# First loads of a transformer kernel re-queued: key weights on ScalarE's DMA queue, x blocks and q0 on SyncE's, with holds

## Chip, cores, metric

The kernel runs on one core of a Trainium2 chip. The metric is device time in microseconds (us) of one execution, as the median over the executions of a round. A profile of one execution gives its span (first to last instruction), which is about 1.8 us less than the device time. "Landed" is the moment when a transfer's completion is signalled.

Engines: PE is TensorE (matmuls), PEld its weight loads, DVE is VectorE, ACT is ScalarE, POOL is GpSimd, SP is SyncE. The loads told of here are issued by SP and ACT (in the profile of before from 0.74 and 0.76 us on); SP's queue is q1 in the profile and ACT's q10.

## The reference, cut to what matters

Four layers over x of 2048 rows by 1024 columns (bfloat16): linear attention, gated MLP, and both again.

```python
x = x + _A_ref(_layernorm(x), A_wqkv, A_wo)          # linear attention
x = x + _B_ref(_layernorm(x), W_gate, W_up, W_down)  # gated MLP
x = x + _A_ref(_layernorm(x), A_wqkv, A_wo)
x = x + _B_ref(_layernorm(x), W_gate, W_up, W_down)
```

Only the start of the first layer matters here: layer-norm of the first four x blocks (128 rows each, x0 to x3) and their products with the two halves of the key weights, k0 and k1 (columns 0 to 511 and 512 to 1023 of the keys).

## The kernel before

The head of the first layer issues the loads and then interleaves, block by block, statistics and scaling on VectorE, transposes and matmuls on TensorE.

```python
# head(): ten idle matmuls on zeros first, then the loads
k0, k1, v0, q0, q1 = (ring.place() for _ in range(5))   # each load goes to SyncE's queue
self.load_x(0, 0, nc.scalar)       # first half of x0, 128 KB
self.load_x(0, 1)                  # second half
self.load_x(1, None, nc.scalar)    # x1, 256 KB
k0(0, H)                           # first half of k0, 512 KB
self.load_x(2, None, nc.scalar)
k0(H, 2 * H)
self.load_x(3, None, nc.scalar)
k1()                               # 1024 KB
q0()
self.load_x(4) ...                 # cut: x5 to x7, q1, x8 to x15, v0
```

```python
# head_units(): the order on each engine, block 0 (x0) and what follows
def block0():
    stat(0, 0); stat(0, 1); rstd(0)      # VectorE; rstd also two steps on ScalarE
    stat(1, 0)                           # x1's statistics fill the wait for rstd(0)
    scale(0, 0); scale(0, 1)             # VectorE
    t0 = turn(0, 0); t1 = turn(0, 1)     # TensorE transposes
    t0("s"); stat(1, 1); rstd(1); t1("v")
    k(0, 0, between)                     # x0 times k0; x1's scaling and transposes in between
# then: block1 = x1 times k0, k(0, 1) = x0 times k1, transposes of x2, k(1, 1), k(2, 0),
# transposes of x3, k(2, 1), k(3, 0), k(3, 1)
```

In all traces here DMAs are issued in the order of their engine's program (SyncE's at 0.74, 1.19 and 1.66 us), and VectorE runs its instructions in the order written, which this kernel fixes by hand. So `scale(0, 0)` doesn't start before `stat(1, 0)` has had x1 (in the first profile of before x1 landed at 5.19, `stat(1, 0)` began at 5.22 and `scale(0, 0)` at 5.90).

Of the kernel before, what the change touches and what calls it, by code (L numbers as in the profile page):

```python
# [18 lines left out]
class _Ring:  # L19
# [9 lines left out]
    def place(self):  # L29

        name, src = self.plan[self.loaded]
        t = self.pool.tile([P, 8, NW], BF16, tag="w")
        self.tiles[name] = t
        self.loaded += 1
        return lambda lo=0, hi=8: self.nc.sync.dma_start(out=t[:, lo:hi, :], in_=src[:, lo:hi, :])

    def load_to(self, n):
        while self.loaded < min(n, len(self.plan)):
# [40 lines left out]
class _Net:  # L79
# [131 lines left out]
    def head(self):  # L211

        nc, tc, ring = self.nc, self.tc, self.ring
        H = self.KT // 2

        zero = self.ep.tile([P, NW], BF16, tag="e")
        nc.vector.memset(zero, 0.0)
        idle = self.ps3.tile([P, NW], F32, tag="b")
        for _ in range(10):
            nc.tensor.matmul(idle, lhsT=zero[:, 0:P], rhs=zero, start=True, stop=True)  # L220

        k0, k1, v0, q0, q1 = (ring.place() for _ in range(5))
        self.load_x(0, 0, nc.scalar)
        self.load_x(0, 1)
        self.load_x(1, None, nc.scalar)
        k0(0, H)
        self.load_x(2, None, nc.scalar)
        k0(H, 2 * H)
        self.load_x(3, None, nc.scalar)
        k1()  # L230
        q0()
        self.load_x(4)
        self.load_x(5)
        self.load_x(6)
        self.load_x(7)
        q1()
        for t in range(8, self.ST):
            self.load_x(t)
        v0()
        src = self.xb  # L240
        self.xnT[0, 0] = self.xnTp.tile([P, self.KT, QT * P], BF16, tag="xnT", name="xnT0_0")
        stats = [self.small.tile([P, 2, nc.vector.BN_STATS_DIM], F32, tag="stats", name=f"st{j}")
                 for j in range(QT)]
        rs, xn = {}, {}

        def stat(j, c):
            self.ln_stat(j, src[j], c, stats[j])

        def rstd(j):
            rs[j] = self.ln_rstd(stats[j])  # L250
            xn[j] = self.xn_home(0, j)

        def scale(j, h=None):
            self.ln_scale(src[j], *rs[j], xn[j], h)

        def turn(j, h):
            tp = self.ps3.tile([P, H, P], BF16, tag="b")
            for i in range(H):
                kt = h * H + i
                nc.tensor.transpose(tp[:, i, :], xn[j][:, kt * P:(kt + 1) * P], self.ident)  # L260
            dst = self.xnT[0, 0][:, h * H:(h + 1) * H, j * P:(j + 1) * P]

            def take(engine):
                if engine == "v":
                    nc.vector.tensor_copy(out=dst, in_=tp)
                else:
                    nc.scalar.activation(out=dst, in_=tp, func=ACT.Copy)

            return take

        return stat, rstd, scale, turn

    def head_units(self, k, stat, rstd, scale, turn):

        def block0():
            stat(0, 0)
            stat(0, 1)
            rstd(0)
            stat(1, 0)
            scale(0, 0)  # L280
            scale(0, 1)
            t0 = turn(0, 0)
            t1 = turn(0, 1)
            t0("s")
            stat(1, 1)
            rstd(1)
            t1("v")
            k(0, 0, between)

        def between():  # L290

            scale(1, 0)
            t0 = turn(1, 0)
            scale(1, 1)
            t0("v")

        def block1():
            turn(1, 1)("v")
            norm(2)
            k(1, 0)  # L300

        def norm(j):
            stat(j, 0)
            stat(j, 1)
            rstd(j)

        def block(j, c, n):
            scale(n)
            t0 = turn(n, 0)
            t1 = turn(n, 1)  # L310
            t0("s")
            t1("s")
            if n + 1 < QT:
                norm(n + 1)
            k(j, c)

        return [block0, block1, lambda: k(0, 1), lambda: block(1, 1, 2), lambda: k(2, 0),
                lambda: block(2, 1, 3), lambda: k(3, 0), lambda: k(3, 1)]

# [62 lines left out]
    def layer_A(self, l, last_ln):  # L382
        nc, G, KT, D = self.nc, self.G, self.KT, self.D
        ring, later = self.ring, self.later
        H = D // NW
# [155 lines left out]
        def column_major(f, q):  # L541
            return [lambda j=j, c=c: f(q, j, c) for c in range(H) for j in range(QT)]
# [4 lines left out]
        def run(*lists):  # L547

            n = max(len(u) for u in lists)
            for i in range(n):  # L550
                for u in lists:
                    if i < len(u):
                        u[i]()
                        later.tick()
# [12 lines left out]
        def quarter0():  # L567
            self.phi_lag = 3 if l == 0 else 0
            run(first)
            run(column_major(q_unit, 0))  # L570
            later.at(1, lambda: None)
            self.phi_lag = 0

        if l == 0:
            with self.tc.manual_schedule(engines={mybir.EngineType.DVE,
                                                  mybir.EngineType.Activation}):
                quarter0()
        else:
            run(first, column_major(q_unit, 0))
# [160 lines left out]
```

## Time and profile before

| | before |
|---|---|
| median of 4 executions (range) | 1629.32 us (1629.21 to 1630.51) |
| the profiled execution: time, span | 1630.68, 1628.9 us |
| TensorE busy | 1621.7 us |
| TensorE idle before the fifth k matmul | 1.73 us, until k0's second half landed |

Read it so: TensorE is full but for some 7 us, so only what moves the start of its unbroken work can move the end. The lines stand in the prediction.

### The profile page before, as it was taken

To read this page: it belongs to the slowest core of one execution; us is meant where nothing else is said; L and a number is where in the kernel's file an instruction comes from. 1 tells how busy PE (TensorE), PEld (TensorE's weight loads), DVE (VectorE), ACT (ScalarE), POOL (GpSimd) and SP (SyncE) were. 2 spreads that over 40 slices of the span, in tenths; PEclk is the share of its full clock that TensorE was granted. 3 is DMA by queue.
4 is the path that set the end of the run, shared out by engine and by line. 5 is a ranking of instruction groups with operands and counts; after the bars stand their busy time and mean duration, and the time that the engine had idled before them with its cause. 6 is when DMAs were issued, how large, how long until landed. Compare 5 with 4: busy or idle time off the path is not lost.

```text
span 1628.9 us, 18772 instructions
## 1 busy us (share of the span) xinstructions
PE 1621.7 (100%) x7754; PEld 739.3 (45%) x7754; DVE 566.7 (35%) x940; ACT 331.8 (20%) x638; POOL 201.9 (12%) x134
## 2 busy tenths in 40 slices
PE   8999999999999999999999999999999999999999
PEld 4444444444444444444444444444444444444444
DVE  7845695213212222212165547942022111111211
ACT  5741212101110110111066312121011101101110
POOL 2349220000000000000023592100000000000000
DMA  7312647448445444544560147464554454454452
GB/s 245 65 52 56 178 71 206 144 148 232 155 143 190 160 151 161 168 147 137 168 128 1 53 93 250 85 193 146 182 165 152 155 184 155 145 166 154 155 162 71
DMA packets 298246, 235.06 MB, mean 144 GB/s; under 512 B 101296, under 2 KB 294192, under 8 KB 298160
## 3 DMA queue, kind: packets, MB, share of 16 engines
q1 hardware_dynamic: 292832, 228.75, 47.7%
q10 hardware_dynamic: 5328, 5.11, 0.9%
q8 instruction: 60, 0.98, 0.3%
q14 instruction: 26, 0.21, 0.0%
HBM read 201.33 MB, written 8.39 MB: 129 GB/s over the span
## 4 chain that ended last, share of the span: by engine, by line
PE 98%; ACT 1%; DVE 1%; DMA 1%; issue 0%; SPq 0%; DVEq 0%
PE pu L639 24%; PE pg L639 24%; PE acc L663 23%; PE ps L404 12%; PE ps L530 7%; PE ps L439 7%; DMA t<-in_A_wqkv_dram 1%; PE kv L452 0%; PE acc_last L663 0%; ACT e L351 0%; ACT e L350 0%; PE fold L515 0%; DVE st L138 0%; ACT e L352 0%; DVE slab L358 0%
## 5 line engine op out<-in xcount | busy, mean ns | idle before, releaser
L639 PEld LDWEIGHTS <-t 128*128 128x128 bf16 x3584 | 350.3, 98 | 423.2
L639 PE MATMUL pu<-xnT,t 128*128 128x512 bf16 x1792 | 423.5, 379 | 0.0
L639 PE MATMUL pg<-xnT,t 128*128 128x512 bf16 x1792 | 423.4, 379 | 0.0
L663 PE MATMUL acc<-t,hT 128*128 128x512 bf16 x1764 | 382.5, 379 | 0.0
L645 DVE TENSOR_TENSOR hT<-pu,rg 128x512 bf16<-128x512 f32 x224 | 154.7, 691 | 572.0 <-PE pu L639 572.0
L644 ACT ACTIVATE rg<-pg 128x512 f32<-128x512 f32 x224 | 133.5, 596 | 737.3 <-PE pg L639 737.0
L663 PEld LDWEIGHTS <-hT 128*128 128x128 bf16 x1820 | 177.9, 98 | 209.1
L404 PE MATMUL ps<-t,xnT 128*128 128x512 bf16 x1024 | 224.3, 380 | 2.2 <-DMA t<-in_A_wqkv_dram 1.7
L404 PEld LDWEIGHTS <-xnT 128*128 128x128 bf16 x1024 | 99.2, 98 | 122.3 <-issue 4.3
L530 PE MATMUL ps<-T,pqT 128*128 128x512 bf16 x512 | 111.2, 379 | 0.0
L145 ACT ACTIVATE rstd<-mv,eps 128x1 f32<-128x1 f32 x64 | 18.7, 293 | 334.1 <-DVE mv L143 333.9
L680 DVE TENSOR_TENSOR xo<-x,acc 128x512 bf16<-128x512 f32 x31 | 21.3, 688 | 170.3 <-PE acc L663 170.3
L483 POOL TENSOR_TENSOR prod<-pq,zrow 128x1024 f32<-128x1024 bf16 x32 | 67.9, 2122 | 85.9 <-DVE den L488 72.5
L138 DVE BATCH_NORM_STATS2 stats<-x 128x6 f32<-128x512 f32 (+1 forms) x120 | 78.0, 673 | 0.8
L530 PEld LDWEIGHTS <-pqT 128*128 128x128 bf16 x512 | 49.9, 98 | 60.4 <-issue 0.5
L419 POOL CAST ksum<-x 128x512 f32<-128x512 bf16 x2 | 1.7, 866 | 605.4 <-DVE x L358 605.4
L677 DVE TENSOR_TENSOR x<-x,acc 128x512 f32<-128x512 f32 x32 | 21.6, 675 | 138.5 <-PE acc L663 137.4
L421 POOL TENSOR_TENSOR ksum<-ksum,slab 128x512 f32<-128x512 f32 x46 | 54.0, 1183 | 84.6 <-DVE slab L358 75.1
L358 DVE SCALAR_TENSOR_TENSOR pq<-ps,e 128x512 bf16<-128x512 f32 x64 | 44.0, 688 | 53.9 <-ACT e L352 52.2
L495 POOL TENSOR_TENSOR pq<-pq,den 128x1024 bf16<-128x1024 bf16 x32 | 61.7, 1933 | 3.1 <-DVE den L490 3.1
L488 DVE TENSOR_REDUCE den<-prod 128x32 f32<-128x1024 f32 x32 | 39.0, 1217 | 53.9 <-POOL prod L483 53.9
L439 PE MATMUL ps<-slab,x 128*128 128x512 bf16 x256 | 56.6, 379 | 0.0
(57 smaller groups left out, 596.0 us busy)
## 6 DMA issues: line engine op xcount, KB each, us to landing
t<-in_B_W_gate_dram SPq DMA_DIRECT2D x56, 1024.0 KB, 7.1
t<-in_B_W_up_dram SPq DMA_DIRECT2D x56, 1024.0 KB, 5.4
t<-in_B_W_down_dram SPq DMA_DIRECT2D x64, 896.0 KB, 5.2
t<-in_A_wqkv_dram SPq DMA_DIRECT2D x11, 1024.0 KB, 5.6
t<-in_A_wo_dram SPq DMA_DIRECT2D x4, 1024.0 KB, 7.2
away<-x SPq DMA_DIRECT2D x8, 512.0 KB, 4.4
x<-away SPq DMA_DIRECT2D x8, 512.0 KB, 8.5
out_dram<-xo ACTq DMA_DIRECT2D x31, 128.0 KB, 2.5
```

The source lines that it names most:

```text
L138: self.nc.vector.bn_stats(out=stats[:, c, :], in_=src[:, c * fmax:(c + 1) * fmax])
L358: nc.vector.scalar_tensor_tensor(out=out, in0=ps, scalar=0.0, in1=e, op0=ALU.max, op1=ALU.add)
L404: nc.tensor.matmul(by_row(ps), lhsT=self.xnT[l, l_q][:, kt, j * P:(j + 1) * P], rhs=w[:, kt, :].rearrange("p (b i d) -> p i b d", i=R, d=H ...
L421: nc.gpsimd.tensor_tensor(out=ksum[:, cols], in0=ksum[:, cols], in1=pk, op=ALU.add)
L439: nc.tensor.matmul(ps, lhsT=self.xn[l, t][:, d * P:(d + 1) * P], rhs=self.pk[l, t][:, h * NW:(h + 1) * NW], start=(t == 0), stop=(t == sel ...
L483: nc.gpsimd.tensor_tensor(out=prod, in0=pq_of[sc, j], in1=zrow, op=ALU.mult)
L495: nc.gpsimd.tensor_tensor(out=heads(pq), in0=heads(pq), in1=den[:, :].unsqueeze(2).to_broadcast([P, D // HD, HD]), op=ALU.mult)
L530: nc.tensor.matmul(ps, lhsT=pqT[sc][:, g, j * P:(j + 1) * P], rhs=T[g // 2][:, g % 2, n2 * NW:(n2 + 1) * NW], start=(g == 0), stop=(g == G ...
L639: nc.tensor.matmul(ps, lhsT=w[:, kt, fi * P:(fi + 1) * P], rhs=self.xnT[l, q][:, kt, :], start=(kt == 0), stop=(kt == KT - 1))
L644: nc.scalar.activation(out=rg, in_=pg, func=ACT.Relu)
L645: nc.vector.tensor_tensor(out=h[:, fi, :], in0=pu, in1=rg, op=ALU.mult)
L663: nc.tensor.matmul(ps[:, 0:n], lhsT=hT[ft // 4][:, ft % 4, j * P:(j + 1) * P], rhs=wd[:, k, i * n:(i + 1) * n], start=(ft == 0), stop=(ft ...
```

## The change

Its intent: k0 should not have to share the DMA engines with x2 and x3, which are needed later (in the profile of before SyncE's queue moved 0.44 MB from 5.5 to 8 us and ScalarE's 0.43). So k0 and k1 get ScalarE's queue, held by a tiny memset into k0's tile until the first x block is on its way; the first x blocks have SyncE's; x2 is held by a memset into its tile that VectorE runs only after the first statistics of x0. In the same move q0 comes directly behind x3 on SyncE's queue, where it used to stand behind k1.

```diff
         k0, k1, v0, q0, q1 = (ring.place() for _ in range(5))
-        self.load_x(0, 0, nc.scalar)
+        self.load_x(0, 0)
         self.load_x(0, 1)
-        self.load_x(1, None, nc.scalar)
-        k0(0, H)
-        self.load_x(2, None, nc.scalar)
-        k0(H, 2 * H)
-        self.load_x(3, None, nc.scalar)
-        k1()
-        q0()
-        self.load_x(4)
...
+        self.load_x(1)
+
+        nc.vector.memset(ring.get((0, "k0"))[:, 0, 0:2], 0.0)
+        k0(0, H, nc.scalar)
+        k0(H, 2 * H, nc.scalar)
+        k1(0, 2 * H, nc.scalar)
+
+        def rest():
+            nc.vector.memset(self.xb[2][:, 0:2], 0.0)
+            self.load_x(2)
+            self.load_x(3)
+            q0()
+            for t in range(4, 8):
+                self.load_x(t)
...
         def block0():
             stat(0, 0)
+            rest()
             stat(0, 1)
```

(Cut: passing `rest` and the queue argument through, and SyncE in the list of engines whose order is kept by hand.)

More of the change, by code (lines that the diff above doesn't have):

```diff
@@ L34, in place @@
         self.loaded += 1
-        return lambda lo=0, hi=8: self.nc.sync.dma_start(out=t[:, lo:hi, :], in_=src[:, lo:hi, :])
+        return lambda lo=0, hi=8, queue=None: (queue or self.nc.sync).dma_start(
+            out=t[:, lo:hi, :], in_=src[:, lo:hi, :])
     def load_to(self, n):
@@ L222, in head @@
         k0, k1, v0, q0, q1 = (ring.place() for _ in range(5))
-        self.load_x(0, 0, nc.scalar)
+        self.load_x(0, 0)
         self.load_x(0, 1)
-        self.load_x(1, None, nc.scalar)
-        k0(0, H)
-        self.load_x(2, None, nc.scalar)
-        k0(H, 2 * H)
-        self.load_x(3, None, nc.scalar)
-        k1()
-        q0()
-        self.load_x(4)
-        self.load_x(5)
-        self.load_x(6)
-        self.load_x(7)
-        q1()
-        for t in range(8, self.ST):
-            self.load_x(t)
-        v0()
+        self.load_x(1)
[10 more added lines that the diff above has]
+                self.load_x(t)
+            q1()
+            for t in range(8, self.ST):
+                self.load_x(t)
+            v0()
         src = self.xb
@@ L269, in turn, with head_units @@
             return take
-        return stat, rstd, scale, turn
-    def head_units(self, k, stat, rstd, scale, turn):
+        return rest, stat, rstd, scale, turn
+    def head_units(self, k, rest, stat, rstd, scale, turn):
         def block0():
             stat(0, 0)
+            rest()
             stat(0, 1)
@@ L574, in layer_A @@
         if l == 0:
-            with self.tc.manual_schedule(engines={mybir.EngineType.DVE,
+            with self.tc.manual_schedule(engines={mybir.EngineType.DVE, mybir.EngineType.SP,
                                                   mybir.EngineType.Activation}):
```

## The prediction

> **What bounds the kernel now.** I read the page first, then the chain that ended last, then TensorE's timeline and the DMA view of the first 20 us. The page says that TensorE is busy for the whole span:
>
> ```profile
> span 1628.9 us, 18772 instructions
> PE 1621.7 (100%) x7754; PEld 739.3 (45%) x7754; DVE 566.7 (35%) x940; ACT 331.8 (20%) x638; POOL 201.9 (12%) x134
> PE 98%; ACT 1%; DVE 1%; DMA 1%; issue 0%; SPq 0%; DVEq 0%
> ```
>
> PE lacks 1628.9 - 1621.7 = 7.2 us, and the ten idle matmuls of the first 5.8 us count as busy though they compute nothing. The change touches only the first loads, so it can win only in the head, before PE runs without a break. By engine and stretch (PE, PEld, DVE, ACT, POOL busy):
>
> ```profile
> 0.00:10.00 10.00, 6.21 (x22) 2.20 (x23) 5.12 (x15) 2.88 (x6) 0.70 (x6) 1.00 0.81 275
> 10.00:20.00 10.00, 9.69 (x62) 4.83 (x62) 8.35 (x17) 4.89 (x12) 2.80 (x3) 1.00 1.08 361
> 20.00:45.00 25.00, 24.89 (x116) 11.19 (x115) 21.40 (x42) 20.64 (x44) 5.90 (x6) 1.00 0.63 167
> ```
>
> From 20 us on PE is full (24.89 of 25.00). So the change of the total is how far the transposes of x block 3, at 19.28 us, move. TensorE's timeline of the head:
>
> ```profile
> 7.46 1.04 PE L404 MATMUL ps<-t,xnT 128*128 128x512 bf16 x4 [0.37 <-ACT xnT L267]
> 10.23 0.59 PE L404 MATMUL ps<-t,xnT 128*128 128x512 bf16 x2 [1.73 <-DMA t<-in_A_wqkv_dram]
> 11.56 3.74 PE L404 MATMUL ps<-t,xnT 128*128 128x512 bf16 x16
> 15.13 0.61 PE L260 MATMUL tp<-ident,x 128*128 128x128 bf16 x8
> 15.58 3.62 PE L404 MATMUL ps<-t,xnT 128*128 128x512 bf16 x16
> 19.28 0.62 PE L260 MATMUL tp<-ident,x 128*128 128x128 bf16 x8
> ```
>
> Four matmuls run with the first half of k0 (x block 0). Then PE stands for 1.73 us until the second half of k0 has landed, at 10.19. The 16 matmuls at 11.56 are block 1 with k0 and, from the ninth on (11.56 + 8 x 3.74/16 = 13.43), block 0 with k1. The chain of waits shows what follows the stall:
>
> ```profile
> 1.66 8.53 DMA t<-in_A_wqkv_dram
> 11.74 0.42 DVE xnT L265
> 12.16 1.20 DVE st L138 x2
> 18.72 0.51 DVE x L154
> 19.28 0.62 PE tp L260 x8
> ```
>
> So from 11.74 VectorE is the chain (transposed copy, statistics and scaling of x2 and x3, the two phi steps of k) until 19.28.
>
> When each load landed, asked for each issue by itself (issue start, time to landing): x0's halves 0.74 + 2.8 = 3.57 and 3.75; x1 1.19 + 4.0 = 5.19; first half of k0 1.19 + 4.5 = 5.73; second half 1.66 + 8.5 = 10.19; x2 9.34; x3 10.45; k1 2.20 + 11.2 = 13.37; q0 16.35. **k1 landed at 13.37 and PE came to it at 13.43.** It was just in time, which no wait in the page tells.
>
> [...] With both queues at work (5.5 to 8 us):
>
> ```profile
> DMA packets 672, 0.87 MB, mean 347 GB/s; under 512 B 35, under 2 KB 463, under 8 KB 672
> q1 hardware_dynamic: 439, 0.44, 51.3%
> q10 hardware_dynamic: 233, 0.43, 46.6%
> ```
>
> With SyncE's queue (q1) alone (11 to 13.4 us) it is 348 GB/s: one rate, 340 KB per us[...]. k0's packets are 1 KB, those of whole x blocks 2 KB[...]. [...]
>
> **The change part by part.**
> (a) Two memsets of two elements on VectorE. The eps memset of about the same width took 0.06 us; together 0.12 us, one before x0 lands (free), one in the statistics of x0 (at most 0.06 us on the path).
> (b) x0 and x1 on SyncE in order. x0's first half is still issued at 0.74 but needn't share; I say it lands 0.2 us earlier, near 3.4 to 3.5. x1 is issued third, near 1.6 instead of 1.19, and lands near 5.2 as before. VectorE needs it right after x0, so the first matmuls stay near 7.2 to 7.5.
> (c) k0 and k1 on ScalarE. The hold is a memset that follows those ending at 1.28; issue near 1.4, 1.85, 2.3 (0.45 each). First half of k0: x0, x1 and it are 1024 KB, as before, so it lands near 5.8. No loss: it is needed at 7.2 or later.
> (d) x2 and x3 held until VectorE has done the first half of x0: about 3.5 + 0.65 + 0.06 = 4.2, issue near 4.4 and 4.8, flowing from about 6.2 (x1 took near 2 us from issue to flow). So the second half of k0 has the rate nearly to itself: from about 5.2, 512 KB / 330 = 1.6 us, data there at 6.8 to 7[...]: lands 7.5 to 9, needed near 8.5. **The 1.73 us stall goes, all or most of it.** x2 lands near 9.5, needed at 12.08 - 1.73 = 10.35.
> (e) But q0 (1024 KB) now follows x3 on SyncE and competes with k1, which before stood ahead of it in the same queue. Before, by the end of k1, x0 to x3, k0 and k1 had moved: 3072 KB, at 340 KB per us from about 2.2, so near 11.2 on average; the landing at 13.37 is 2.1 later[...]. After: by 6.2 ScalarE's queue has moved some 860 KB[...]. Landing 0.6 to 2 us later, **14.0 to 15.4 instead of 13.37.**
> Sum: PE reaches k1 at 13.43 - 1.73 = 11.7 and then waits until it lands. Between k1 and 19.28 PE itself waited only about 0.4 us (0.32 of it before x2's transposes), and VectorE's chain, now ahead, no longer binds. So the gain is the smaller of 1.73 and 13.43 + 0.4 - (landing of k1): with 14.0 to 15.4 it is -0.2 to -1.6; with some chance that q0 comes into play late, I take the middle at -0.3. **Predicted: 1629.3 + 0.3 = 1629.6 us.**
>
> **The rivals.**
> 1. *The stall is simply gone.* If q0 doesn't hold k1 back[...], k1 lands by 12.1 and the whole 1.73 us is gained: 1627.6. For it: in the trace x2 on the second queue began only after the first half of k0 was done, so queues don't always share at once, and q0's own issue took 1.39 instead of 0.4 us. Against: from 5.5 on they shared.
> 2. *k1 takes the place of k0 as the wait* (my choice). For it: 13.37 against 13.43. Full lag: 1630.9.
> 3. *x2 becomes the wait.* Held to 4.4 and taking 7.7 us from issue to landing as before, it would land at 12.1, VectorE's chain would stand where it was, and nothing is gained: 1629.3.
> 4. *Nothing beyond the head.* Later loads move the same bytes, and the built program has the same order of instructions on PE, GpSimd and, but for the memsets and loads, on the others; I see no way to more than 2 or 3 us either way.
>
> **Range and chances.** Full gain 1627.6 and full loss 1630.9 are the ends of the mechanism; the runs of before spread by 1.3 us (1629.21 to 1630.51). Range 1627.5 to 1631.4. Two per cent is 33 us, more than the whole head is long: faster 0.01, same 0.98, slower 0.01.
>
> **What would show it right or wrong.** In the profile after: the wait of 1.73 us before the fifth k matmul gone or under 0.5; in its place a PE wait on the k weights 16 matmuls in, ending between 13.9 and 15.5 (k1's landing); x3's transposes between 19.3 and 20.5; q0 and k1 flowing at the same time in the DMA view of 9 to 13 us; x2 landed by 10.3. It is wrong if k1 lands before 13, if PE waits for x2's scaling instead, or if the second half of k0 still lands after 9.5.

Passages are cut from this text where no trace shows what they say of the hardware; the steps that hung on them were the author's assumption. Two terms of the sum: in (d), allowances that led from data at 6.8 to 7 to a landing at 7.5 to 9; in (e), an assumed division of the rate between the two queues, by which the data of k1 had moved by 13.4. With them the sum came to k1 landing at 14.0 to 15.4, a gain of -0.2 to -1.6 us, taken at -0.3, and so to 1629.6 us. The 330 KB per us in (d) is an estimate from the 347 and 348 GB/s of the two stretches. "Near 2 us from issue to flow" is 2.3 to 2.4 in the trace: x1 was issued at 1.19, and ScalarE's queue moves packets of 2 KB from between 3.5 and 3.6 us on.

## More of the kernel before

The mean clock is the share of TensorE's full clock that was granted over an execution. All executions told here are of the state "fast".

## The result, and the profile after

| | before | after |
|---|---|---|
| median of 4 executions | 1629.32 us | 1631.47 us |
| range | 1629.21 to 1630.51 | 1631.17 to 1632.02 |
| span of the profiled execution | 1628.9 us | 1629.7 us |

The ratio is 1.0012, 95% interval 0.9995 to 1.0029. A ratio here is the mean time of one kernel's fast runs over that of the other's of the same rounds, so not quite the ratio of the medians. By the 2% rule the two are the same; but the slowest of four executions of before is faster than the fastest of four after, and the traces account for it, once before has been profiled a second time (e1).

The head of the page after, for the whole span:

```profile
span 1629.7 us, 18774 instructions
PE 1622.8 (100%) x7754; PEld 740.4 (45%) x7754; DVE 566.5 (35%) x942; ACT 331.8 (20%) x638; POOL 201.9 (12%) x134
```

TensorE is busy for 1.1 us longer though it runs the same 7754 matmuls: some of them ran slower. TensorE's timeline of the head after (start, length, line and tiles, count; in brackets the idle time before and what ended it):

```profile
7.50 0.72 PE L265 MATMUL tp<-ident,x 128*128 128x128 bf16 x8 [2.04 <-DVE x L155]
8.59 2.74 PE L410 MATMUL ps<-t,xnT 128*128 128x512 bf16 x6 [0.37 <-ACT xnT L272]
...
12.33 3.62 PE L410 MATMUL ps<-t,xnT 128*128 128x512 bf16 x16
15.92 0.62 PE L265 MATMUL tp<-ident,x 128*128 128x128 bf16 x8
...
20.08 0.62 PE L265 MATMUL tp<-ident,x 128*128 128x128 bf16 x8
```

The wait of 1.73 us for k0 is gone, as intended: six matmuls follow each other. But the first one starts at 8.59 instead of 7.46, because TensorE had nothing for 2.04 us before x0's transposes, and the six take 2.74 us where in the second profile of this kernel (e11) they take 1.47. x3's transposes start at 20.08, 0.80 later than in the profile before, which is the whole difference of these two spans (1629.7 - 1628.9).

VectorE's timeline says what the 2.04 us waited for:

```profile
4.95 0.21 DVE L144 BATCH_NORM_AGGREGATE mv<-st 128x2 f32<-128x12 f32 x1
6.43 0.69 DVE L139 BATCH_NORM_STATS2 st<-x 128x6 f32<-128x512 bf16 x1 [1.27 <-DMA x<-in_A_x_dram]
7.04 0.72 DVE L155 TENSOR_SCALAR x<-x,mv,rstd 128x512 bf16<-128x512 bf16 x2
```

x0's statistics were ready at 5.16. The next instruction in VectorE's order is x1's first statistics, and x1 landed only at 6.41 (before: 5.19). x0's scaling stands behind it.

The slow matmuls show in the view by stretches, whose figure before the last two is the clock granted to TensorE:

```profile
5.00:8.40 3.40, 1.17 (x10) 0.45 (x8) 2.09 (x5) 0.96 (x3) 0.00 (x0) 1.00 1.08 367
8.40:11.80 3.40, 3.21 (x11) 1.46 (x12) 1.24 (x5) 0.63 (x3) 0.00 (x0) 0.50 1.08 361
```

After a stretch in which TensorE was busy for 1.17 of 3.40 us its clock was half for the next 3.4 us: the trace's record of the clock has it at half from 8.40 to 11.81, 3.41 us.

And k1, which the prediction feared for: landed at 13.74 (2.36 + 11.4), TensorE reached it at 14.06. No wait shows, because everything ahead of it had become later.

### The profile page after: what moved, and what is told of

The parts are those of the page before. It is cut to its first block, busy times and chain, and to the rows that moved or that the text cites. A ratio compares the mean times of both kernels' runs of the same rounds, so it can differ in the third digit from the quotient of the medians.

```text
span 1629.7 us, 18774 instructions
## 1 busy us (share of the span) xinstructions
PE 1622.8 (100%) x7754; PEld 740.4 (45%) x7754; DVE 566.5 (35%) x942; ACT 331.8 (20%) x638; POOL 201.9 (12%) x134
## 4 chain that ended last, share of the span: by engine, by line
PE 98%; ACT 1%; DVE 1%; DMA 0%; issue 0%; SPq 0%; DVEq 0%
PE pg L645 24%; PE pu L645 24%; PE acc L669 23%; PE ps L410 12%; PE ps L536 7%; PE ps L445 7%; PE kv L458 0%; PE acc_last L669 0%; DMA x<-in_A_x_dram 0%; ACT e L357 0%; ACT e L356 0%; PE fold L521 0%; DVE st L139 0%; ACT e L358 0%; DVE slab L364 0%
```

## The experiments

Theories, after the first comparison. **A**: there are two costs, one behind the other. x1 lands later, VectorE's order makes x0 wait for it, TensorE idles and its clock falls to half; and k1, delayed by q0, would be the next wait. **B**, my prediction's: k1 delayed by q0 is all that costs. **C**, about the baseline: the first profile of before caught a slow execution. Later, on why x1 is late, **D**: k0, issued just before it on the other queue, goes first; **E**: being third on its own queue is what delays it.

The same numbers from each profile, in us. "k1 wait" is TensorE's idle time before x0 times k1; "x3" is the start of x3's transposes. Landings are from asking for each issue by itself. Waits for k0 stand in the timelines: 1.73 us in the first profile of before, 1.04 in e7, 0.35 in e9, 0.62 and 0.41 in e12 (one for each half). e1 to e4 and e9 to e11 ran on one chip, e5 to e8 on a second and e12 on a third; each was run beside before on the same chip, and medians are to be compared within these sets.

| kernel | x1 landed | k0 whole | k1 landed | first k matmul | k1 wait | x3 | span | median |
|---|---|---|---|---|---|---|---|---|
| before, first profile | 5.19 | 10.19 | 13.37 | 7.46 | none | 19.28 | 1628.9 | 1629.32 |
| after | 6.41 | 7.92 | 13.74 | 8.59 | none | 20.08 | 1629.7 | 1631.47 |
| e1 before again | 5.29 | 8.76 | 11.66 | 7.67 | none | 17.84 | 1627.5 | 1629.49 |
| e2 x1 first on ScalarE | 4.33 | 8.06 | 13.36 | 7.84 | 1.45 | 19.02 | 1628.6 | 1630.66 |
| e3 scale x0 first | 6.04 | 7.81 | 13.73 | 6.67 | 1.68 | 19.40 | 1629.0 | 1630.86 |
| e4 19 idle matmuls | 6.69 | 8.07 | 14.05 | 8.87 | 1.11 | 19.71 | 1629.6 | 1631.64 |
| e5 k1 ahead of q0 | 6.37 | 8.03 | 12.40 | 8.54 | none | 20.15 | 1629.8 | 1630.74 |
| e6 = e3 and e5 | 6.31 | 7.63 | 12.30 | 6.95 | none | 17.97 | 1627.6 | 1629.48 |
| e7 before, q0 on ScalarE | 5.27 | 9.47 | 15.47 | 7.44 | 2.76 | 22.80 | 1632.4 | 1633.44 |
| e8 = e5 and k0 after x1 | 4.99 | 7.99 | 12.39 | 7.38 | 0.94 | 18.05 | 1627.7 | 1629.75 |
| e9 = e8, k1 ahead of x3 | 4.68 | 8.49 | 12.17 | 7.07 | 0.44 | 17.84 | 1627.4 | 1629.19 |
| e10 before, x2 and x3 on SyncE | 5.66 | 7.14 | 10.83 | 7.83 | none | 17.76 | 1627.4 | 1629.17 |
| e11 after again | 6.06 | 7.88 | 13.41 | 8.23 | 1.11 | 19.08 | 1628.7 | 1631.55 |
| e12 = e10, all on SyncE | 4.70 | 8.53 | 12.47 | 7.13 | 0.71 | 18.14 | 1627.7 | 1629.52 |

In every row span minus x3 is 1609.6 us (1609.9 in e4). So nothing after the start of x3's transposes differs between the profiled executions, and for them the column x3 is the whole story.

The 95% intervals of the ratios are some 0.13% to either side, 2 us: only e4's and e7's lie above 1.0 altogether. The verdicts below rest on where waits stand in the traces and on whole sets of executions, not on the ratios alone.

### e1: the kernel before, once more

No edit. The median of before and its first profile did not fit together (the profiled execution is 1.4 us slower than the median), so it was profiled again.

> The kernel before, unchanged, profiled a second time. Its profiled execution took 1630.68 us while most of its executions took 1629.3, so its profile may show an unlucky one. If so (theory C): a span near 1627.5, the second half of k0 landing near 9 instead of 10.19, a PE wait near 0.5 instead of 1.73, x3's transposes near 18 instead of 19.28. If not: the same 1.73 us wait and 19.28, and a span of 1628.9. Ratio to before 1.000 either way.

Measured: 1629.49 (1629.25 to 1630.45); ratio 1.0002. The profiled execution took 1629.25. TensorE's timeline in it:

```profile
7.67 1.72 PE L404 MATMUL ps<-t,xnT 128*128 128x512 bf16 x6 [0.47 <-ACT xnT L267]
...
10.13 3.63 PE L404 MATMUL ps<-t,xnT 128*128 128x512 bf16 x16
...
17.84 0.62 PE L260 MATMUL tp<-ident,x 128*128 128x128 bf16 x8
```

Six matmuls nearly in one run, and x3's transposes 1.44 us earlier than in the first profile. The six take 1.72 us, 0.25 more than in e11: so much of the wait for k0 is left, as its second half landed at 8.76. **Of the stall of 1.73 us that the change was to remove, all but some 0.25 us is absent in this execution.** k0's second half landed at 8.76 instead of 10.19 and k1 at 11.66 instead of 13.37, with the same program. Of the 36 executions of before that were run beside the experiments, 27 took 1629.14 to 1629.88 and 9 took 1630.40 to 1631.04; the first profile (1630.68) was one of the slower kind. Some of these have a mean clock of 0.999 and some 1.000, so more than one thing puts an execution there; the runs don't settle which.

### e2: x1 first on ScalarE's queue

```diff
-        self.load_x(1)
+        self.load_x(1, None, nc.scalar)
```

> The changed kernel, but x1 is issued first on ScalarE's queue, ahead of k0, as before the change. Theory A (x1 issued third lands 1.2 us later, holds up VectorE's statistics that stand ahead of x0's scaling, PE idles 2 us, and its clock falls to half): x1 lands by 5.0, first k matmul near 7.2 instead of 8.59, six matmuls at full clock, block 1's matmuls near 10.9 instead of 12.33; then the wait for k1 (landed 13.74) shows, near 1 us, and the time is about 1630.9; if k1 doesn't bind, 1629.7. Theory B (my prediction: k1's late landing is what costs): 1631.5, unchanged.

Measured: 1630.66 (1629.67 to 1631.83); ratio 1.0008. x1 landed at 4.33, the mean clock is 1.000 in all five executions, and TensorE then met this:

```profile
10.05 1.90 PE L410 MATMUL ps<-t,xnT 128*128 128x512 bf16 x8
13.40 1.89 PE L410 MATMUL ps<-t,xnT 128*128 128x512 bf16 x8 [1.45 <-DMA t<-in_A_wqkv_dram]
...
19.02 0.61 PE L265 MATMUL tp<-ident,x 128*128 128x128 bf16 x8
```

Block 1 with k0 began at 10.05, 2.3 us earlier than after; then TensorE stood 1.45 us for k1. So there are two costs in a row, and the first hides the second. A price of this arrangement: x0, now sharing with x1, landed at 4.09 and 4.72 instead of 2.78 and 4.20.

### e3: VectorE scales x0 before it touches x1

```diff
             rstd(0)
-            stat(1, 0)
             scale(0, 0)
             scale(0, 1)
             t0 = turn(0, 0)
             t1 = turn(0, 1)
             t0("s")
+            t1("v")
+            stat(1, 0)
             stat(1, 1)
             rstd(1)
-            t1("v")
```

> The changed kernel, loads untouched, but VectorE scales and copies x0 before it touches x1, so a late x1 (6.4 us) no longer holds up block 0. Theory A: first k matmul near 7.1 instead of 8.59, no half clock, x1's transposes near 10, block 1 near 10.7 instead of 12.33, then a wait for k1 until 13.7: time about 1630.9. Theory B: 1631.5, unchanged. If the clock falls all the same (PE idle between 5.45 and 6.2 in any case), near 1631.5 with slow matmuls.

Measured: 1630.86 (1630.80 to 1633.09); ratio 1.0013. The loads are those of after and x1 still landed at 6.04, but the first k matmul came at 6.67. The time is what theory A gave: a late x1 costs only through the order on VectorE, and k1 takes over:

```profile
13.78 1.89 PE L410 MATMUL ps<-t,xnT 128*128 128x512 bf16 x8 [1.68 <-DMA t<-in_A_wqkv_dram]
```

### e4: 19 idle matmuls instead of 10

```diff
-        for _ in range(10):
+        for _ in range(19):
```

> The changed kernel with 19 idle matmuls instead of 10, so that PE stays busy until x0 is ready at 7.5. The late x1 stays. Theory A: first k matmul still at 8.59, but at full clock: the first six in 1.3 instead of 2.5 us, block 1 near 11.0 instead of 12.33, then a wait for k1 of near 1 us until 13.7; time about 1630.9; if k1 doesn't bind, 1630.2. If idling has nothing to do with the slow matmuls: 1631.5, and 420 ns between the first six matmuls as now.

Measured: 1631.64 (1631.38 to 1632.24); ratio 1.0014. The six matmuls took 1.47 us instead of 2.74, and all five executions have a mean clock of 1.000, where six of the nine of after have less. So with TensorE kept busy up to 7.5 us the clock stayed full. The time did not fall as expected: in this profile x1 landed at 6.69 and k1 at 14.05, each some 0.3 later than after, and TensorE waited 1.11 us for k1. Here the clock alone was not worth having while k1 was late.

### e5: k1 ahead of q0 on SyncE

```diff
-        k1(0, 2 * H, nc.scalar)
...
             self.load_x(3)
+            k1()
             q0()
```

> The changed kernel, but k1 on SyncE's queue behind x3 and ahead of q0, so q0 no longer competes with it; x1's late landing stays. Theory A (two costs side by side: late x1 with the half clock, and late k1): k1 lands near 11.7 to 12.2 instead of 13.74, but PE comes to it only at 13 to 14, so x3's transposes stay near 19.5 to 20 and the time near 1631.2. Theory B (k1 against q0 alone is what costs): near 1629.5.

Measured: 1630.74 (1629.60 to 1632.04); ratio 1.0006. k1 landed at 12.40 and nobody waited for it. The executions fall in two groups: 1629.60 and 1629.73 with a mean clock of 1.000; 1630.74, 1631.55 and 1632.04 with 0.999. The profiled one is of the second group; half a clock for 3.41 us of 1630 is a mean of 0.999. So with k1 out of the way these executions are 1.4 to 2.7 us above the median of before (1629.36 in these rounds) where the clock fell, and 0.2 to 0.4 above where it didn't. Only one of the five was profiled, so how late x1 was in the others isn't known. That the clock alone makes this difference is not shown: e5 with 19 idle matmuls, which would show it, was not run. Neither theory's number was right for all executions: A's holds for three, B's for two.

### e6: e3 and e5 together

The edit is the two diffs above in one kernel.

> Both costs taken away: VectorE scales x0 before it touches x1 (as in e3_scale_first), and k1 stands ahead of q0 on SyncE's queue (as in e5_k1_sync). Theory A: k1 lands near 12, PE comes to it at 12.0, no wait of 1.68 us, x3's transposes near 17.6 (17.84 in the second profile of before), time 1629.2, level with before. Theory B: the same. If a third cost stands behind them: 1630 or more, like e3_scale_first's 1630.86.

Measured: 1629.48 (1629.37 to 1629.60); ratio 0.9999. x3's transposes at 17.97; k1 landed at 12.30, just as TensorE came to it (12.35). With both costs taken away the change is level with before, so no third one of any size is hidden behind them. The four kernels after, e3, e5 and e6 are the four combinations of the two costs: 1631.5, 1630.9, 1630.7 and 1629.5.

### e7: one part alone, in the kernel before

```diff
         k1()
-        q0()
+        q0(0, 2 * H, nc.scalar)
```

> The kernel before with one part alone: q0 on ScalarE's queue behind x3, so that it competes with k1 on SyncE's. Nothing else is moved. Theory A and B: k1 lands near 13.4 to 14 instead of 11.66, PE waits for it some 1.5 to 2 us after block 1, x3's transposes near 19.4 instead of 17.84, time 1630.8 to 1631.3. If sharing the queues does not hold k1 back: 1629.4.

Measured: 1633.44 (1631.78 to 1634.22); ratio 1.0022, interval 1.0009 to 1.0034. k1 landed at 15.47, and q0 at 15.64, side by side:

```profile
15.51 3.07 PE L404 MATMUL ps<-t,xnT 128*128 128x512 bf16 x8 [2.76 <-DMA t<-in_A_wqkv_dram]
```

Letting q0 flow beside k1 delays k1 by 3.8 us against e1, and by 2.1 against the first profile of before, which had landed it late by itself. I had expected 2; my number was taken over from after, where k1 had a start on q0. After the wait of 2.76 us the clock fell once more (half from 16.05 to 19.47), which explains why the eight matmuls took 3.07 us instead of 1.89.

### e8: k0 issued after x1

e5 with a longer hold:

```diff
-        nc.vector.memset(ring.get((0, "k0"))[:, 0, 0:2], 0.0)
+        nc.vector.memset(ring.get((0, "k0"))[:, 2:5, :], 0.0)
```

> The changed kernel with k1 on SyncE ahead of q0 (as in e5_k1_sync), and k0 held 0.8 us longer (a memset of three row blocks of it instead of two elements), so x1 is issued before k0, still third on SyncE. Tells why x1 lands late. Theory D (k0's first half, issued 0.3 us before x1 on the other queue, goes first): x1 lands near 4.6 instead of 6.41, k0's halves near 7 and 8.4, first k matmul near 7.1, block 1 near 9.6, x3's transposes near 17.3, time 1629.0. If x1's place third on its own queue is the cause (theory E): x1 still lands after 6, time near 1631.

Measured: 1629.75 (1629.44 to 1630.14); ratio 1.0001. x1 is still the third load on SyncE's queue, issued at 1.66 as after; only k0, on the other queue, is issued at 2.12 instead of 1.34. x1 landed at 4.99 instead of 6.41 (6.37 in e5, from which e8 differs by the hold alone). It isn't chance: the six profiles with the short hold and x1 on SyncE have 6.04 to 6.69, the two with the long one (e8, e9) 4.99 and 4.68. So **x1 is late because a transfer of 512 KB was issued on the other queue 0.3 us before it**, not because of its place in its own queue. The time missed what I expected, 1629.0: TensorE now waited 0.94 us for k1, and x3's transposes came at 18.05, not 17.3. The DMA view shows the same from the side of the packets. Between 3.0 and 4.2 us after (q10 holds k0, q1 holds the end of x0 and x1):

```profile
q10 hardware_dynamic: 259, 0.27, 72.0%
q1 hardware_dynamic: 18, 0.01, 3.2%
```

and in the same stretch of e1, where q10 holds x1:

```profile
q1 hardware_dynamic: 275, 0.28, 66.1%
q10 hardware_dynamic: 92, 0.17, 37.1%
```

The same stretch in e8, and in the second profile of after (e11):

```profile
q1 hardware_dynamic: 123, 0.22, 59.0%
q10 hardware_dynamic: 45, 0.05, 23.6%
```

```profile
q10 hardware_dynamic: 216, 0.22, 58.0%
q1 hardware_dynamic: 56, 0.11, 25.8%
```

In the first profile of after, SyncE's queue moves hardly anything in this stretch, 18 packets beside 259. In e11 the two share, 56 beside 216, and x1 landed late all the same (6.06). So k0 needn't shut x1 out; an unfavourable share makes x1 late too. In e8, with k0 issued later, x1 goes first. How the share is decided stays open.

### e9, e10, e12: tries at beating both

e9 is e8 with k1 one place earlier:

```diff
             self.load_x(2)
-            self.load_x(3)
             k1()
+            self.load_x(3)
```

e10 is the kernel before with x2 and x3 in SyncE's one queue (the diff below), and e12 is e10 with `nc.scalar` taken from the loads of x0 and x1 too:

```diff
         k0(0, H)
-        self.load_x(2, None, nc.scalar)
         k0(H, 2 * H)
-        self.load_x(3, None, nc.scalar)
+        self.load_x(2)
         k1()
+        self.load_x(3)
         q0()
```

> A try at beating both: e8_x1_ahead with k1 ahead of x3 on SyncE (x3 is needed at 13.0, k1 at 11.5). Theory: k1 lands near 11.7 instead of 12.39, x3 near 12.4, the wait of 0.94 us for k1 falls to 0.2 or less, and VectorE's chain (statistics of x2 at 10.1) sets x3's transposes near 17.4: time 1629.0, 0.4 us under before. If x3 comes too late, VectorE waits for it and the time stays at 1629.5.

> The same order of arrival without holds: the kernel before, with x2 and x3 moved from ScalarE's queue to SyncE's in the order k0, x2, k1, x3, q0[...]; x0's first half and x1 stay on ScalarE. Theory: second half of k0 lands near 7.9 instead of 8.76, x2 8.7, k1 11.7, x3 12.4; block 1 near 9.4 instead of 10.13, x3's transposes near 17.2 instead of 17.84: time 1628.9. If the order of the queue does not matter: 1629.4.

> The last try at beating both, and the test of the order alone: e10_one_queue with x0's first half and x1 moved to SyncE as well, so every early load stands in one queue in the order of need: x0, x1, k0, x2, k1, x3, q0, with no hold anywhere. Theory: x1 lands near 4.8 (5.66 in e10_one_queue), k0's halves near 6.1 and 7.6, k1 near 11.2; first k matmul near 7.1, block 1 near 9.4, x3's transposes near 17.1 to 17.4; most executions 1628.6 to 1628.9. If the third issue on one queue costs more than it saves (x1 after 5.5): as e10_one_queue, 1629.2.

Measured: e9 1629.19 (1628.62 to 1629.30), ratio 0.9994; e10 1629.17 (1628.71 to 1630.50), ratio 0.9998; e12 1629.52 (1628.65 to 1630.46), ratio 1.0000; all intervals hold 1. e9's five executions lie within 0.7 us; of before's nine beside it four took 1629.25 to 1629.32 and five 1630.50 to 1630.61. That is a hint of a few tenths, no more. In e9's profile TensorE still waited 0.44 us for k1 (0.2 or less was expected) and x3's transposes came at 17.84, not 17.4. In e10 the weights landed even earlier than expected (k0 at 7.14, k1 at 10.83), but x1 came at 5.66 and held VectorE up for 0.57 us, and most of the gain was gone. In e12 x1 came at 4.70, but k0 and k1 0.9 and 1.3 us later than expected. Each arrangement wins at one load and pays at another: x0 to x3, k0 and k1 are 3 MB, and nearly all of it is needed by 13 us.

### e11: the changed kernel, once more

> The changed kernel unchanged, for a second profile on the same chip as the tries. Theory A: x1 lands after 6, first k matmul after 8.4; where the mean clock is 0.999, six matmuls at half clock and a span near 1629.7; where it is 1.000, a wait for k1 until about 13.8 instead and a span of 1629.3 to 1629.6. Median 1631.5.

Measured: 1631.55 (1630.47 to 1633.18); ratio 1.0012. The profiled execution was the fastest, and its clock stayed full:

```profile
8.23 1.47 PE L410 MATMUL ps<-t,xnT 128*128 128x512 bf16 x6 [0.37 <-ACT xnT L272]
...
13.46 1.89 PE L410 MATMUL ps<-t,xnT 128*128 128x512 bf16 x8 [1.11 <-DMA t<-in_A_wqkv_dram]
...
19.08 0.61 PE L265 MATMUL tp<-ident,x 128*128 128x128 bf16 x8
```

With a full clock TensorE comes to k1 early and waits for it, as predicted (the span, 1628.7, is below the 1629.3 to 1629.6 that I expected for this case); with half a clock (first profile) it comes late and there is nothing left to wait for. Either way it is later than e1: by 1.24 us here (19.08 - 17.84) and by 2.24 there.

What went before a fall of the clock can be laid out from the traces. Each trace's record of the clock changes at multiples of 3.41 us (e7: full for 10.24, half for 3.41), so each trace can be divided into windows of 3.41 us from the record's first entry on. Up to that entry (4.37 us in e3, 7.28 in e9) the idle matmuls start 0.43 us apart, twice the 0.22 of a full clock (eight k matmuls in 1.90 us in e2), though the view prints a clock of 1.00 there. From that entry on, three windows were followed by a half clock, and TensorE was busy in them for 1.18 us (after, 4.99 to 8.40), 1.27 (e5) and 0.65 (e7). The least busy window that no half clock followed is one of e3, and e11's window around its idle 1.35 us is above it too (the number behind 3.41 is TensorE's busy time):

```profile
11.20:14.61 3.41, 1.73 (x9) 0.68 (x7) 3.31 (x8) 0.98 (x3) 0.85 (x1) 1.00 1.10 353
5.95:9.36 3.41, 1.84 (x14) 0.99 (x15) 2.93 (x8) 1.09 (x3) 0.00 (x0) 1.00 1.07 372
```

So in these twelve profiles (the first of before and e12 have no record) the windows before a half clock had 0.65 to 1.27 us of work and all others 1.73 or more. The single gaps part in the same way: 2.04 us (after), 1.77 us (e5) and 2.76 us (e7) were each followed by 3.41 us at half clock; 1.45 us (e2), 1.68 us (e3) and 1.73 us (the first profile of before) were not. Which of the two counts is not shown: no run tested it by moving the work, and no window had between 1.27 and 1.73.

## Why the prediction was right or wrong

**What bounds the kernel: right.** Span minus the start of x3's transposes is 1609.6 to 1609.9 us in all fourteen profiles; the change acts in the head alone.

**(a) The memsets: right.** 0.06 us each, the second at 3.44 beside a wait for x0.

**(b) x0 and x1 on SyncE: the step that failed.** The prediction has "x1 is issued third ... and lands near 5.2 as before", and so "the first matmuls stay near 7.2 to 7.5". x1 landed at 6.41 (6.06 in e11), the first k matmul came at 8.59 (8.23). I took x1 to get the share that it had before, when it and k0 were issued at the same moment (1.19); k0, issued 0.3 us earlier on the other queue, was ahead of it (e8). The prediction's rival 1 had noted that x2 on the second queue began only after the first half of k0 was done (from 4.85 to 5.65 us q10 moved 7 packets beside q1's 252; that half landed at 5.73), and (b) made no use of it. x0's first half came sooner than I said, at 2.78, which helped nobody; its second half came at 4.20 in one profile and 3.31 in the other (3.75 before). That a late x1 stops x0 by VectorE's order was in the program, and e3 shows it.

**A term that the sum had not at all: the clock.** After the idle time that (b) made, TensorE's clock fell to half for 3.41 us; six of the nine executions of after have a mean clock under 1.000. What it costs by itself is not separated. The two profiles of after differ by 1.0 us in span and e5's two groups by 1.0 to 2.4, but x1's landing differs as well; and the executions of after at 1.000 took 1631.46, 1631.38 and 1630.47, most of the others 1631.2 to 1632.0. Where k1 is late too, a full clock wins little (e4).

**(c) First half of k0: off, without effect.** 6.56 instead of 5.8 (5.86 in e11); needed at 8.59.

**(d) Second half of k0: the mechanism right, its worth wrong.** It landed at 7.92, inside 7.5 to 9, and the wait is gone. But "the 1.73 us stall" that was to be won belongs to a slow execution. In an ordinary one (e1) only some 0.25 us of it is there to win. This is the second step that failed, by its size. I had paired the profile of a 1630.68 us execution with a median of 1629.3. The mismatch stood in the table.

**(e) q0 against k1: right in kind, off in the landing.** 14.0 to 15.4 predicted, 13.74 and 13.41 measured. The foretold wait for k1, ending between 13.9 and 15.5, is not in the first profile, where TensorE came later than k1, and ended at 13.46 in e11. Between 9.5 and 12 us after, the two queues moved packets in equal number:

```profile
q1 hardware_dynamic: 417, 0.46, 56.7%
q10 hardware_dynamic: 415, 0.42, 51.8%
```

The lines for 5.5 to 8 us in the prediction show sharing too, but not equal numbers: 439 packets beside 233, for 0.44 and 0.43 MB. Against an ordinary execution of before the delay is 1.8 to 2.1 us (13.4 to 13.7 against 11.66), the upper end of the 0.6 to 2 that I gave. It is TensorE's wait in e11, and by itself it cost most in e7.

**The sum.** x3's transposes were foretold between 19.3 and 20.5 and came at 20.08 and, in e11, at 19.08, outside. Median foretold 1629.6, range to 1631.4; measured 1631.47, just above the upper end. Of the 1.9 us between, 1.4 is the base: x3 at 19.28 belongs to a span of 1628.9, but the median that I added to belongs to 1627.5. The rest, about 0.5, is the late x1 and the clock, less what I had put too high for k1. By medians, k1's delay without the late x1 costs 1.3 to 1.5 us (e2 and e3 against before), and the late x1 some 0.6 more (after against e3). The verdict "same" could hardly fail, since 2% is 33 us. The direction holds because of (e); the way there held in one of its two halves.

**The rivals.** Rival 1 (all gained) is refuted: k1 was late in both profiles. Rival 2 is what e2, e3, e4 and e11 show. Rival 3 (x2 becomes the wait) is refuted: x2 landed at 9.93 and VectorE came to it at 12.88. Rival 4 is right.

## What to carry to other kernels

Before a stall in a profile is worked on, see that the profiled execution is an ordinary one: compare its time with the median, and profile twice. When a load is moved to another queue, list for every load what now stands ahead of it and beside it, on both queues, down to the last one needed; here the load that had been just in time (k1) and the one that VectorE touched next in its fixed order (x1) paid for the one that was favoured. Idle times of TensorE of 1.77 to 2.76 us (after, e5, e7) cost twice here, by the wait and by the 3.41 us of half clock after it.
